# Mask products of an attention kernel moved from score tiles of their own into unused columns

## The chip, the cores and the metric

The kernel runs on one NeuronCore of a Trainium2 chip. The metric is the device time of one execution in microseconds (us), lower is better.

## What is computed

Three stages, one after the other, all in fp32:

```python
# attention: B, H, S, D = 2, 8, 768, 64, 16 centroids per head
q_assign = argmax(einsum('bhsd,hcd->bhsc', q_n, c_n))      # nearest centroid of each query
k_assign = argmax(einsum('bhsd,hcd->bhsc', k_n, c_n))      # and of each key
mask = q_assign[:, :, :, None] == k_assign[:, :, None, :]
scores = where(mask, q @ k.T / 8, -1e9)
attn = softmax(scores) @ v
# layer 1: 1536 tokens, 512 -> 2048 -> 512, a rational function between
# layer 2: 1536 tokens, 512 -> 1024 -> 512, softmax, normalisation between
```

Only the attention is touched by the change. A mask is made of the assignments: every query and every key gets a row of 16 zeros and ones (one-hot), and these rows are added to the operands of the score product, so that pairs of another cluster come out very low.

## The kernel before, in words

**Units.** The attention is a loop over 96 units (line 745): 16 heads n, 6 tiles of 128 queries t, idx = 6n + t. A unit makes its scores with four matmuls (L410 twice, L416 twice) in a PSUM tile `s` of two banks of 512 columns, of which it uses 384 each (`unit_scores`, L402). VectorE takes the minimum of each row (L421, called the max below, the sign being turned), ScalarE the exponential (L433, the exp below). At each odd unit VectorE transposes the exponentials of the two units before (L461, 1.77 us). TensorE multiplies them with v (L473); at t = 1 ScalarE copies the product of an earlier head out in two pieces (L491). The tiles `s` are a ring of two buffers: a unit's scores can be written when the tile two places earlier in the ring has been read out.

**Heads.** While head n runs, GpSimd prepares the operands of head n+1 (`prep_head`, L369 to L387): it needs the loads `dup` of that head (`load_head`, L213), issued on SP's queue at t = 3 of head n-1. At its fifth step SP copies the one-hot rows of the head into the operands (L386, L387).

**Masks.** They are made for sets of heads. Sets 0 and 1 are made at the start, sets 2, 3 and 4 (four heads each) inside the loop, by `assign` (L585), at the units listed in `SLOTS` (L105), after their queries and keys were loaded (`load_pairs`, L200, at the unit in `PAIRS`, L107: set 3 at unit 17, set 4 at 40). The steps of a set:

1. Three units hold the products with the centroids (L286) in columns 384 to 511 of their own score tiles, ahead of the scores; ScalarE copies them out after the exp of that unit (`keep`, L295).
2. `turn_in`: six transposes (L299) in a tile of their own; VectorE finds the maximum and compares (`is_max`, L305, L306).
3. `turn_back`: six bf16 transposes (L319) in a tile of their own; ScalarE copies 768 columns out (`back`, L323).
4. `first`: the product with a triangular matrix (L329) in a tile of its own; ScalarE copies 768 columns out (`to_rows`, L334), GpSimd turns half of the rows over (L336).

A tile of its own takes one place in the ring of two. Steps put in `pre` run on TensorE ahead of the unit's score matmuls, which are then ordered behind them (L407 to L414). `sums_out` (L511) also uses `pre`, at units 15, 27, 39, 51 and so on.

The instructions of an engine run in the order in which the program's scheduler has put them; `issue_after` and `behind` set parts of that order. Weights of the first layer are converted beside the attention (`to_f32`, L149 to L157): ScalarE's part for each piece comes every six units, at 29, 35, 41, 47, 53.

Of the kernel before, what the change touches and what calls it, by code (L numbers as in the profile page):

```python
# [7 lines left out]
F32 = mybir.dt.float32  # L8
F32R = mybir.dt.float32r
BF16 = mybir.dt.bfloat16  # L10
AF = mybir.ActivationFunctionType
ALU = mybir.AluOpType
# [3 lines left out]
B, H, S, D = 2, 8, 768, 64  # L16
C = 16
NT = S // 128
# [12 lines left out]
def fused_kernel(ctx: ExitStack, tc: tile.TileContext, qT, kT, v, cent, w1, w2i, w2o, gln, coef, centT, cst, tri, out):  # L31
    nc = tc.nc
# [14 lines left out]
    def psum2(tag, name):  # L47
        return ps[tag].tile([128, 2, 512], F32, name=name, tag=tag, bufs=2)
# [5 lines left out]
    def bank(tag, name):  # L54
        return stp.tile([128, 512], F32, name=name, tag=tag)
# [14 lines left out]
    trib = asp.tile([128, 128], BF16, name="trib")  # L70
    one = [asp.tile([128, 1], F32, name=f"one{i}") for i in range(2)]
# [30 lines left out]
    ACL = 67  # L102
    SET1 = (3, 5, 7)
    NBUSY = 15
    SLOTS = {2: (9, 10, 11, 12, 13, 15), 3: (24, 26, 28, 30, 31, 33), 4: (48, 50, 52, 54, 55, 57)}  # L105
    CONV, PARTS, SPLIT = 29, (69, 69, 81, 81, 87, 87, 89, 89, 93, 95), (39, 45, 63, 63)
    PAIRS = {17: 3, 40: 4}  # L107

    OLAG = 2

# [58 lines left out]
    def w1_f32(f):  # L169
        for a in range(2):  # L170
            o = slice(512 * a, 512 * a + 512)
            yield from to_f32(w1_f[f][:, o], w1[f, :, o], f"w1{f}{a}", True)

    def early_raws(f):
        for a in range(2):
            load_raw(w1[f, :, 512 * a:512 * a + 512], f"w1{f}{a}")
            yield
# [62 lines left out]
    t = bank("a0", "warm")  # L240
# [23 lines left out]
    MS, E, FV, FT, OH = {}, {}, {}, {}, {}  # L264

    def scales(k):
        es = sets[k]
        m = sm.tile([128, 3], F32, name=f"msc{k}", tag="msc", bufs=2)
        for j, (pp, i) in enumerate(es):
            if k < 1:  # L270
                nc.gpsimd.memset(m[32 * j:32 * j + 32, 0:1], 1.0 if i else -BIG)
                nc.gpsimd.memset(m[32 * j:32 * j + 32, 1:2], 0.0 if i else BIG)
            p = pp % 4
            (nc.vector if k < 1 else nc.gpsimd).tensor_copy(m[32 * j:32 * j + 32, 2:3], cnr[32 * p:32 * p + 32])
        OH[k] = qk.tile([128, S], F32R, name=f"oh{k}", tag="oh", bufs=2)
        for j, (pp, i) in enumerate(es):
            for h in range(2):
                mk[2 * pp + h, i] = OH[k][32 * j + 16 * h:32 * j + 16 * h + 16]
        MS[k] = m

    def sims(k, t0, nt, o):

        n = 128 * nt
        for j, (pp, i) in enumerate(sets[k]):
            p = pp % 4
            r = nc.tensor.matmul(o[32 * j:32 * j + 32], lhsT=cT[:, p * 32:(p + 1) * 32], rhs=raw["p", pp, i][:, t0 * 128:t0 * 128 + n])  # L286
        return r

    def keep(k, t0, nt, o):
        M = 32 * len(sets[k])  # L290
        if k not in E:
            E[k] = asp.tile([128, S], F32, name=f"sm{k}", tag="sm", bufs=2)
            FV[k] = asp.tile([128, NT, M], BF16, name=f"f{k}", tag=f"f{k > 1}", bufs=1 + (k < 2))
            FT[k] = E[k].bitcast(BF16)[:, 0:S]
        return nc.scalar.activation(out=E[k][0:M, t0 * 128:(t0 + nt) * 128].rearrange("p (a n) -> p a n", n=o.shape[2]), in_=o[0:M], func=AF.Copy, scale=MS[k][0:M, 2:3])  # L295

    def by_token(k, t, o):
        M = 32 * len(sets[k])
        return nc.tensor.transpose(o, E[k][0:M, t * 128:(t + 1) * 128], ident[0:M, 0:M])  # L299
# [18 lines left out]
    def mask_t(k, t, o):  # L318
        return nc.tensor.transpose(o, FV[k][:, t], identb)  # L319


    def back(k, o):
        nc.scalar.activation(out=FT[k][0:o.shape[0]], in_=o, func=AF.Copy)  # L323

    def first(k, o):

        M = 32 * len(sets[k])
        for a in range(2):
            nc.tensor.matmul(o[0:M, a, 0:384], lhsT=trib[0:M, 0:M], rhs=FT[k][0:M, 384 * a:384 * a + 384])  # L329

    def to_rows(k, o):

        M = 32 * len(sets[k])
        nc.scalar.activation(out=OH[k][0:M].rearrange("p (a n) -> p a n", a=2), in_=o[0:M], func=AF.Relu, scale=one[k > 1][0:M])  # L334
        q = OH[k][0:M // 2]
        nc.gpsimd.tensor_scalar(q, q.bitcast(F32), -1.0, 1.0, op0=ALU.mult, op1=ALU.add)  # L336
        masked[k] = S

    masked = dict.fromkeys(range(len(sets)), 0)
# [60 lines left out]
    pre, steps = {}, {}  # L400
# [39 lines left out]
    def step(u, e, f):  # L440
        steps.setdefault((u, e), []).append(f)
# [143 lines left out]
    def assign(k, us):  # L585

        w = {}

        def slot(i):
            w[i] = psum2("s", f"w{k}{i}")  # L590
            return w[i]

        def two_sims(c):
            def g(sp):
                w[c] = sp[:, :, 384:512]
                for t in range(2):
                    r = sims(k, 2 * c + t, 1, sp[:, t, 384:512])
                return r
            return g

        def turn_in():
            o = slot(3)
            for t in range(NT):
                by_token(k, t, o[:, t // 3, t % 3 * 128:t % 3 * 128 + 128])

        def turn_back():
            o = slot(4).bitcast(BF16)[:, 0]
            for t in range(NT):
                mask_t(k, t, o[:, t * 128:t * 128 + 128])

        step(us[0] - 1, "dve", lambda: scales(k))
        for c in range(3):
            pre[us[c]] = [two_sims(c)]
            step(us[c], "act", lambda c=c: keep(k, 2 * c, 2, w[c]))
        step(us[3], "pe", turn_in)
        step(us[3], "dve", lambda: is_max(w[3][:, :, 0:384], FV[k].rearrange("p (a t) m -> p a (t m)", a=2)))
        step(us[4], "pe", turn_back)
        step(us[4], "act", lambda: back(k, w[4].bitcast(BF16)[:, 0, 0:S]))
        step(us[5], "pe", lambda: first(k, slot(5)))
        step(us[5], "act", lambda: to_rows(k, w[5][:, :, 0:384]))  # L620

    scales(0)
    M = 32 * len(sets[0])
# [15 lines left out]
    for a in range(2):  # L639
        tps.append(bank(f"a{a}", f"set0{a}")[:, 0:3 * M].rearrange("p (t m) -> p t m", t=3))  # L640
        for t in range(3):
            r = by_token(0, 3 * a + t, tps[a][:, t])
        is_max(tps[a], EQ[:, 3 * a:3 * a + 3])
    t = bank("b1", "busy")
    for i in range(NBUSY):
        w = nc.tensor.matmul(t[:, 0:128], lhsT=z, rhs=z)
# [10 lines left out]
    for i in range(2):  # L657
        for a in (i, 1 - i):
            c = slice(384 * a, 384 * a + 384)
# [4 lines left out]
    for a in range(2):  # L664
        c = slice(384 * a, 384 * a + 384)
# [42 lines left out]
    for k in range(2, len(sets)):  # L708
        assign(k, SLOTS[k])
    for f in range(NPRE):  # L710
        w1_f[f] = wl0.tile([128, 1024], F32, name=f"w1f{f}", tag="l")
    for f in range(NPRE):
        g = w1_f32(f)
# [4 lines left out]
        g = early_raws(f)  # L718
        for a in range(2):
            planc[CONV - 6 + 12 * f + 6 * a].append(g)  # L720
        g = w1_parts(f)
# [23 lines left out]
    for idx, (n, t) in enumerate(units):  # L745
# [9 lines left out]
        with tc.issue_after(last["mk", n].ins) if n else ExitStack(), tc.issue_after(last["v"].ins) if n > 1 else ExitStack():  # L755
            if idx in PAIRS:
                load_pairs(sets[PAIRS[idx]])
            if t == 3 and 0 < n < B * H - 2:
                load_head(n + 2)
        sp = unit_scores(n, t)  # L760
# [313 lines left out]
    for f in (*range(NPRE, 16), *(16 + i for i in (0, 1, 2, 3, 6, 7, 4, 5))):  # L1074
        for a in range(2):
            if f < 16:
                to_load.append((w1[f, :, 512 * a:512 * a + 512], f"w1{f}{a}"))
            else:
                c = 2 * (f - 16) + a
# [93 lines left out]
```

## Time and profile before

| what | us |
|---|---|
| median of 3 runs | 635.71 (635.43 to 636.82) |
| the profiled execution, its own time | 632.73 |
| its span, first to last instruction | 630.9 |
| first exp of the 96 units starts | 17.09 |
| last exp of the 96 units starts | 211.13 |

Times in the rows are counted from the start of the span. A row of a timeline has start, duration, engine, line, operation, output and inputs, and in brackets how long the engine was idle before it and what ended that. Consecutive instructions of one group are one row with their count.

### The profile page before, as it was taken

The page shows a single profiled execution, that of the slowest core. Times are in us where ns is not written, and L with a number is a line of the kernel's source. Part 1 is how long each engine was busy: PE and PEld are TensorE (multiplying, and loading weights), DVE is VectorE, ACT ScalarE, POOL GpSimd, SP SyncE. Part 2 cuts the span into 40 slices and gives each one's busy share as a digit, 9 for nine tenths or more (in the row PEclk, how much of TensorE's full clock was granted, in tenths as well). Part 3 has the DMA queues.
Part 4 walks back from the last instruction along what each step waited for, and adds up shares of the span by engine and source line. Part 5 has one row for each costly group of instructions (what it writes and reads, how often), then busy time and mean ns, then how long its engine had stood idle before and what let it go on. Part 6 is the DMA issues. An engine that isn't in the chain of part 4 may idle for free.

```text
span 630.9 us, 13931 instructions
## 1 busy us (share of the span) xinstructions
PE 596.7 (95%) x5591; PEld 473.2 (75%) x5591; DVE 479.9 (76%) x633; ACT 444.2 (70%) x811; POOL 394.4 (63%) x338
## 2 busy tenths in 40 slices
PE   8789898989897999999999999999999999999997
PEld 5466666657675877888888888877888888888886
DVE  4888889989999798979889768689797554453450
ACT  4766678768787889899898787989794344443342
POOL 7845488788989679989989886888784000000000
PEclk9999999999999999999999999999999999999999
DMA  9948969977984523223313232221000000000001
GB/s 229 218 102 240 232 173 269 218 186 193 228 188 120 166 70 106 89 68 100 101 66 102 66 78 90 67 72 62 2 0 1 1 18 33 18 18 33 18 17 51
DMA packets 22585, 64.80 MB, mean 103 GB/s; under 512 B 4548, under 2 KB 5784, under 8 KB 22520
## 3 DMA queue, kind: packets, MB, share of 16 engines
q1 hardware_dynamic: 22088, 63.73, 37.3%
q8 instruction: 44, 0.72, 0.5%
q10 hardware_dynamic: 432, 0.17, 0.1%
q14 instruction: 21, 0.17, 0.1%
HBM read 59.23 MB, written 3.19 MB: 99 GB/s over the span
## 4 chain that ended last, share of the span: by engine, by line
PE 61%; POOL 11%; ACT 9%; DVE 8%; DMA 6%; issue 3%; SPq 2%; POOLq 0%; ACTq 0%; DVEq 0%
PE y L922 16%; PE h L815 15%; PE hh L1010 11%; PE o L1061 10%; DMA dup<-in_kT 4%; DVE m L421 2%; PE pv L473 2%; ACT p L433 2%; POOL k L377 2%; PE s L410 2%; POOL q L382 2%; PE lt L1043 2%; DMA raww<-in_w 1%; DVE pt L461 1%; PE s L416 1%
## 5 line engine op out<-in xcount | busy, mean ns | idle before, releaser
L433 ACT ACTIVATE p<-s,m 128x768 f32<-128x768 f32 x96 | 86.2, 900 | 49.4 <-DVE m L421 48.7
L815 PE MATMUL h<-xhl,w1h 128*128 128x512 f32 x336 | 106.5, 393 | 0.1
L421 DVE TENSOR_REDUCE m<-s 128x1 f32<-128x768 f32 x96 | 88.4, 941 | 17.1 <-PE s L416 17.1
L473 PE MATMUL pv<-pt,v 32*64 32x192 f32 x3072 | 81.0, 330 | 4.7 <-ACT w L491 4.7
L461 DVE STREAM_TRANSPOSE pt<-p 128x1536 f32<-128x1536 f32 (+1 forms) x49 | 84.9, 1732 | 0.2 <-ACT p L433 0.2
L905 POOL TENSOR_TENSOR gl<-y,gh 128x512 fp32r<-128x512 f32 x48 | 71.3, 1488 | 16.7 <-ACT gh L904 16.5
L473 PEld LDWEIGHTS pv<-pt,v 32*64 32x64 f32 x3072 | 57.9, 130 | 22.0 <-issue 13.5
L815 PEld LDWEIGHTS h<-xhl,w1h 128*128 128x128 f32 x336 | 62.8, 188 | 14.8 <-DVE y L899 0.5
L410 PE MATMUL s<-k,q 128*128 128x384 f32 x192 | 57.4, 381 | 12.7 <-ACT p L433 8.3
L922 PE MATMUL y<-gl,w1h 128*128 128x512 f32 x168 | 66.1, 393 | 1.3 <-POOL gl L905 1.3
L886 POOL TENSOR_TENSOR q<-q,t 128x512 f32<-128x512 f32 x48 | 64.4, 1343 | 2.9
L922 PE MATMUL y<-gh,w1l 128*128 128x512 f32 x168 | 65.8, 392 | 0.0
L815 PE MATMUL h<-xhl,w1l 128*128 128x512 f32 x168 | 65.6, 392 | 0.0
L922 PE MATMUL y<-gh,w1h 128*128 128x512 f32 x168 | 61.7, 392 | 0.0
L410 PEld LDWEIGHTS s<-k,q 128*128 128x128 f32 x192 | 29.3, 188 | 33.5 <-ACT p L433 16.2
L885 POOL TENSOR_SCALAR q<-t,ab 128x512 f32<-128x512 f32 x48 | 42.4, 884 | 17.9 <-ACT t L883 13.0
L1010 PE MATMUL hh<-vh,xhl 128*128 128x512 f32 x160 | 51.0, 395 | 0.0
L887 DVE TENSOR_TENSOR y<-y,h 128x512 f32<-128x512 f32 x48 | 32.8, 684 | 23.4 <-ACT y L884 23.1
L416 PE MATMUL s<-k,q 128*128 128x384 f32 x192 | 49.3, 338 | 0.3 <-DVE k L663 0.3
L897 DVE SCALAR_TENSOR_TENSOR q<-q,h 128x512 f32<-128x512 f32 x47 | 32.1, 682 | 11.7 <-ACT h L895 11.0
L922 PEld LDWEIGHTS y<-gl,w1h 128*128 128x128 f32 x168 | 31.5, 188 | 9.6 <-POOL gl L905 2.8
L904 ACT ACTIVATE gh<-y 128x512 fp32r<-128x512 f32 x48 | 30.0, 631 | 11.6 <-DVE y L899 11.5
(189 smaller groups left out, 1414.5 us busy)
## 6 DMA issues: line engine op xcount, KB each, us to landing
raww<-in_w SPq DMA_DIRECT2D x32, 512.0 KB, 3.6
v<-in_v SPq DMA_DIRECT2D x64, 192.0 KB, 4.1
dup<-in_qT SPq DMA_DIRECT2D x31, 192.0 KB, 5.9
dup<-in_kT SPq DMA_DIRECT2D x31, 192.0 KB, 5.9
rawv<-in_w2i SPq DMA_DIRECT2D x8, 512.0 KB, 3.5
rawv<-in_w2o SPq DMA_DIRECT2D x8, 512.0 KB, 3.7
out<-ob SPq DMA_DIRECT2D x11, 256.0 KB, 2.0
pr<-in_qT SPq DMA_DIRECT2D x7, 384.0 KB, 6.8
```

The lines of the kernel that those rows point to most:

```text
L410: r = nc.tensor.matmul(sp[:, a, 0:384], lhsT=q1[i][:, sl], rhs=k1[i][:, a * 384:(a + 1) * 384], start=True, stop=False)
L416: last["pe"] = nc.tensor.matmul(sp[:, a, 0:384], lhsT=q2[i][:, sl], rhs=k2[i][:, a * 384:(a + 1) * 384], start=False, stop=True)
L421: last["dve"] = nc.vector.tensor_reduce(m, sp[:, :, 0:384], axis=AX.XY, op=ALU.min)
L433: last["act"] = nc.scalar.activation(out=P[n, t // 2][:, t % 2], in_=sp[:, :, 0:384], func=AF.Exp, scale=-1.0, bias=m, accum_out=rs[key][: ...
L461: r = nc.vector.transpose(PT[n][:, 2 * i + m * a:2 * i + m * a + m].rearrange("p t k -> p (t k)"), p[:, m * a:m * a + m].rearrange("p t a ...
L473: last["pv"] = nc.tensor.matmul(pv[n][64 * c:64 * c + 64, r, 0:192].rearrange("p (t q) -> p t q", t=NT), lhsT=vv[n][sl, j], rhs=PT[n][sl, ...
L815: r = nc.tensor.matmul(hp, lhsT=w[:, kt * 128:(kt + 1) * 128], rhs=x[:, kt], start=(i == 0), stop=(i == 11))
L886: nc.gpsimd.tensor_tensor(q, q, t, op=ALU.mult)
L905: nc.gpsimd.tensor_tensor(gl, y, gh.bitcast(F32), op=ALU.subtract)
L922: nc.tensor.matmul(o, lhsT=w[:, c], rhs=g, start=(first and i == 0), stop=(last and i == 2))
L1010: last["th"] = nc.tensor.matmul(hp[:, a], lhsT=y[:, kt], rhs=w[:, 512 * a:512 * a + 512], start=(kt == 0 and e == 0), stop=(kt == 3 and e ...
L1061: r = nc.tensor.matmul(op[:, 0:m], lhsT=l[:, kt], rhs=w, start=(n == 0), stop=(n == 23))
```

## The change

`SLOTS` gets nine units for each set instead of six. The tile of its own stays for `turn_in` alone. The transposes back are made in the spare columns of two units (four and two transposes), the triangular products in those of three units (256 tokens each), all through `pre`, and each is copied out by ScalarE after the exp of its unit: two pieces instead of one, and three instead of one. Set 2 starts at the same unit as before, sets 3 and 4 two units earlier, and their pairs are loaded one unit earlier.

```diff
-    SLOTS = {2: (9, 10, 11, 12, 13, 15), 3: (24, 26, 28, 30, 31, 33), 4: (48, 50, 52, 54, 55, 57)}
+    SLOTS = {2: (9, 10, 11, 12, 13, 14, 16, 17, 18), 3: (22, 24, 26, 28, 29, 30, 31, 32, 33), 4: (46, 48, 50, 52, 53, 54, 55, 56, 57)}
...
-    PAIRS = {17: 3, 40: 4}
+    PAIRS = {16: 3, 39: 4}
...
-        def turn_back():
-            o = slot(4).bitcast(BF16)[:, 0]
-            for t in range(NT):
-                mask_t(k, t, o[:, t * 128:t * 128 + 128])
+        def turn_back(t0, n):
+            def g(sp):
+                w[t0, "b"] = sp.bitcast(BF16)[:, :, 768:1024]
+                for t in range(n):
+                    r = mask_t(k, t0 + t, w[t0, "b"][:, t // 2, t % 2 * 128:t % 2 * 128 + 128])
+                return r
+            return g
+
+        def first_of(c):
+            def g(sp):
+                w[c, "f"] = sp[:, :, 384:512]
+                for t in range(2):
+                    o = 256 * c + 128 * t
+                    r = nc.tensor.matmul(sp[:, t, 384:512], lhsT=trib, rhs=FT[k][:, o:o + 128])
+                return r
+            return g
+
+        def back_of(t0, n):
+            nc.scalar.activation(out=FT[k][:, 128 * t0:128 * (t0 + n)].rearrange("p (a n) -> p a n", n=256), in_=w[t0, "b"][:, 0:n // 2], func=AF.Copy)
+
+        def rows_of(c):
+            o = OH[k][:, 256 * c:256 * c + 256]
+            nc.scalar.activation(out=o.rearrange("p (a n) -> p a n", a=2), in_=w[c, "f"], func=AF.Relu, scale=one[1])
+            q = o[0:64]
+            nc.gpsimd.tensor_scalar(q, q.bitcast(F32), -1.0, 1.0, op0=ALU.mult, op1=ALU.add)
+            masked[k] += 256
...
-        step(us[4], "pe", turn_back)
-        step(us[4], "act", lambda: back(k, w[4].bitcast(BF16)[:, 0, 0:S]))
-        step(us[5], "pe", lambda: first(k, slot(5)))
-        step(us[5], "act", lambda: to_rows(k, w[5][:, :, 0:384]))
+        for i, (t0, n) in enumerate(((0, 4), (4, 2))):
+            pre[us[4 + i]] = [turn_back(t0, n)]
+            step(us[4 + i], "act", lambda t0=t0, n=n: back_of(t0, n))
+        for c in range(3):
+            pre[us[6 + c]] = [first_of(c)]
+            step(us[6 + c], "act", lambda c=c: rows_of(c))
```

## Rows read from the trace of the kernel before

**Rows 1.** The page: bytes moved in 40 slices of 15.8 us, the chain that ended last.

```profile
GB/s 229 218 102 240 232 173 269 218 186 193 228 188 120 166 70 106 89 68 100 101 66 102 66 78 90 67 72 62 2 0 1 1 18 33 18 18 33 18 17 51
...
PE 61%; POOL 11%; ACT 9%; DVE 8%; DMA 6%; issue 3%; SPq 2%; POOLq 0%; ACTq 0%; DVEq 0%
```

**Rows 2.** Timeline of ScalarE: the exps of units 31, 32, 33, 34, 35, 36, 37, 38.

```profile
81.39 0.90 ACT L433 ACTIVATE p<-s,m 128x768 f32<-128x768 f32 x1 [2.05 <-DVE m L421]
...
84.76 0.90 ACT L433 ACTIVATE p<-s,m 128x768 f32<-128x768 f32 x1
...
85.65 0.90 ACT L433 ACTIVATE p<-s,m 128x768 f32<-128x768 f32 x1
...
89.08 0.90 ACT L433 ACTIVATE p<-s,m 128x768 f32<-128x768 f32 x1 [1.65 <-DVE m L421]
...
90.42 0.90 ACT L433 ACTIVATE p<-s,m 128x768 f32<-128x768 f32 x1 [0.35 <-DVE m L421]
...
93.00 0.90 ACT L433 ACTIVATE p<-s,m 128x768 f32<-128x768 f32 x1 [0.37 <-DVE m L421]
...
94.09 0.90 ACT L433 ACTIVATE p<-s,m 128x768 f32<-128x768 f32 x1
...
96.75 0.90 ACT L433 ACTIVATE p<-s,m 128x768 f32<-128x768 f32 x1 [0.16 <-DVE m L421]
```

**Rows 3.** Timeline of VectorE at unit 30 and 31: the compare, the next max.

```profile
79.16 0.96 DVE L306 TENSOR_TENSOR f<-w,mx 128x768 bf16<-128x768 f32 x1
80.40 0.96 DVE L421 TENSOR_REDUCE m<-s 128x1 f32<-128x768 f32 x1 [0.28 <-PE s L416]
```

**Rows 4.** Timeline of TensorE: scores of units 30, 31, transposes back, scores of units 48, 54.

```profile
76.30 0.61 PE L410 MATMUL s<-k,q 128*128 128x384 f32 x2 [0.95 <-DMA dup<-in_kT]
...
79.40 0.62 PE L410 MATMUL s<-k,q 128*128 128x384 f32 x2 [1.48 <-ACT p L433]
...
81.09 0.51 PE L319 MATMUL w<-identb,f 128*128 128x128 bf16 x6
...
113.50 0.62 PE L410 MATMUL s<-k,q 128*128 128x384 f32 x2
...
127.19 0.61 PE L410 MATMUL s<-k,q 128*128 128x384 f32 x2 [1.24 <-POOL q L382]
```

**Rows 5.** Groups of instructions by form: count, busy us, mean ns, idle before.

```profile
L152 ACT ACTIVATE raww<-raww,less 128x512 uint32<-128x512 uint32 x32 | 24.6, 770 | 0.0
...
L491 ACT ACTIVATE w<-pv 64x768 f32<-64x768 f32 x16 | 12.9, 806 | 0.3
...
L149 ACT ACTIVATE w1f<-raww 128x512 f32<-128x512 f32 x10 | 6.6, 664 | 0.0
...
L1065 ACT ACTIVATE ob<-o 128x512 f32<-128x512 f32 x11 | 6.5, 593 | 14.2 <-PE o L1061 14.2
...
L295 ACT ACTIVATE sm<-s,msc 128x256 f32<-128x256 f32 x9 | 4.2, 466 | 0.0
...
L334 ACT ACTIVATE oh<-w,one 128x768 fp32r<-128x768 f32 x3 | 2.7, 893 | 0.0
...
L336 POOL TENSOR_SCALAR oh<-oh 64x768 fp32r<-64x768 f32 x3 | 2.5, 831 | 6.2 <-ACT oh L334 6.2
...
L323 ACT ACTIVATE sm<-w 128x768 bf16<-128x768 bf16 x3 | 2.4, 801 | 0.0
```

**Rows 6.** Tile pr, window 40 to 130: what TensorE waited for before L286 (us, times).

```profile
  ACT sm L295: 2.8, 6
```

**Rows 7.** The chain, window 14 to 150: load of head 8.

```profile
97.98 6.16 DMA dup<-in_kT
```

**Rows 8.** Timeline of SP's queue: first loads of pairs of set 4.

```profile
98.62 1.06 SPq L209 DMA_DIRECT2D pr<-in_qT  x2
```

**Rows 9.** Timeline of GpSimd: first and last instruction of the preparation of head 8.

```profile
104.28 0.91 POOL L363 TENSOR_SCALAR k<-dup,sgn 128x768 fp32r<-128x768 f32 x1 [2.37 <-DMA dup<-in_kT]
...
108.90 1.83 POOL L382 TENSOR_TENSOR q<-dup,q 64x768 fp32r<-64x768 f32 x1
```

## The prediction

> **What bounds the kernel now.** I read the page's chain first, to see which engines carry the end [rows 1]: TensorE has 61%, most of it in the two layers behind the attention, which the change doesn't touch and which start when the attention is done. The rest is the attention, where the chain changes hands between VectorE, ScalarE, GpSimd and loads. So the question is by how much the last unit ends earlier; the layers move with it.
>
> The second view is ScalarE's timeline, where the starts of the exps give the step from unit to unit [rows 2]. Without mask work a step from an odd to an even unit is 2.58 us (35 to 36) or 2.66 where an earlier product is copied out (37 to 38); the reader is to compare 3.37 (31 to 32) and 3.43 (33 to 34), the units behind which the transposes back and the triangular product take a tile of their own. The same steps stand at units 13 and 15, 55 and 57, so each of the three sets pays both. The third view is VectorE and TensorE around the compare [rows 3, 4], for what a matmul that needs the compare's result would wait for. The fourth is the start of heads 5 and 9 (units 30 and 54), where TensorE stands 0.95 and 1.24 us until the head's operands are there, which come late because their loads do [rows 4].
>
> **The sum, term by term.** All of it is against the profiled execution (632.73 us, span 630.9). The median shown is 3.0 us above that, so I work out a difference and take it from the median.
>
> A, the two tiles removed from the ring. Transposes back: 3.37 - 2.66 = 0.71 us. Triangular product: 3.43 - 2.58 = 0.85 [rows 2]. Three sets: **-4.7 us**. The third tile, for turn_in, stays, with VectorE's compare.
>
> B, a new wait. The transposes back now stand on TensorE ahead of the scores of the unit right behind the compare, and those scores are ordered behind them. Before, the next unit's scores needed only the exp: they began at 79.40 and the max at 80.40, while the compare ran until 79.16 + 0.96 = 80.12 [rows 3, 4]. Now TensorE waits for 80.12, makes four transposes (four sixths of 0.51 is 0.34) and then the scores, 1.0 us to the max as before: 81.5. VectorE's next max is 1.1 us later, and queued behind it are its transpose of the exponentials, and on TensorE the unit's products with v, so nothing slips into the gap. If something hid it, it would cost nothing; the bounds are 0 and 1.1 a set. I take the upper, as the rows show all three operations and no other work on VectorE: **+3.3 us**.
>
> C, ScalarE's smaller pieces. The triangular products come out as 3 x 0.466 for one of 0.893, +0.51; the transposes as about 0.59 (512 columns, by the nearest row) and 0.47 (256) for 0.80, +0.26 [rows 5]. That is 0.77 a set. Each piece also holds its unit's tile until it is done: TensorE (its weight loads counted apart) waited 6 times, 0.47 us each, for such copies of spare columns [rows 6]. Were each of the fifteen new copies paid like that, it would be 7.0 us, the upper bound; the lower is 0, where VectorE ends last. I take 0.5 a set, two thirds of ScalarE's growth: ScalarE ends last where the 0.81 us copies of the product with v fall (units 13, 31, 55), VectorE in the others. **+1.5 us**.
>
> D, the moved compare. In sets 3 and 4 turn_in goes from units 30 and 54 to 28 and 52, ahead of the two stalls. The extra time of the compare then passes while the loads are on their way, and up to 0.95 + 1.24 = 2.2 us of stall go [rows 4]. What is late next is ScalarE: between the exps of units 29 and 30 (53 and 54) lie its part of a weight conversion, 0.66 + 0.77 [rows 5], now a copy of 0.59, and the exp with its accumulator read, about 1.0: 3.0 us where 2.6 was the step, 0.4 each back. Net **-1.4 us**, between -2.2 and 0.
>
> E, the loads of pairs one unit earlier. At unit 39 this passes something: the pairs (4 x 393 kB = 1.57 MB) are now issued ahead of head 8's operands, not behind them as in [rows 7, 8]. At the 269 GB/s of that slice [rows 1] 1.57 MB are 5.8 us. Head 8's preparation began at 104.28, waiting for its load, and ended at 108.90 + 1.83 = 110.7 [rows 9]; unit 48's scores, which need it, began at 113.50 [rows 4], a slack of 2.8. So a load 5.8 us later costs 3.0 and one up to 2.8 later nothing. Before, the pairs were already on their way while head 8's load landed, 6.16 us after its last issue, so part of the 5.8 was paid then; I take a delay of 3.3, **+0.5 us**. At unit 16 the pairs pass no other load: nothing, covered by the six units until their first use; if they were late, unit 22's scores would stand behind them.
>
> F, at nothing: the centroid products of sets 3 and 4 move by two units, at the same price. GpSimd's turning over comes in three pieces for one of 0.83 us [rows 5]; it waited 6.2 us for ScalarE there, and the mask is ready by units 18, 33 and 57, three units or more before its rows are copied. If GpSimd were full there, a piece would cost some 0.3 us. VectorE's count of instructions stays.
>
> Sum: -4.7 + 3.3 + 1.5 - 1.4 + 0.5 = **-0.8 us**, 634.9 from the median. About 0.2% (1.3 us) is what a measurement of this kernel can tell from no change, so I forecast no difference that can be told.
>
> **A rule beside term C.** TensorE's waits for copies of spare columns show that a bank isn't written again before the copy has ended, though the columns differ [rows 6]. The Trainium skill, PSUM — Partial Sum Buffer, section "PSUM bank collisions raise a hardware error", says that two engines must be kept off one bank in the same partitions whatever the columns, so unused columns are no room beside the scores but a longer hold on the bank. The trace agrees that there is a wait. By the rule alone every copy is paid, C is 7.0 and the sum +4.7; by the rows' mix of waits and slack it is -0.8.
>
> **The rivals.** *The new wait is hidden (faster).* VectorE's max can slip behind the compare without loss if ScalarE, with its larger load in these units, ends last there anyway; then B is nearly nothing and A stands. For it: before the exps of units 32 and 33 ScalarE wasn't idle [rows 2]. Against: at unit 31 it stood 2.05 us for VectorE's max. With B at zero the sum is -4.1, 631.6; it decides from half of B on (-2.4, 633.3).
>
> *The load of head 8 is held up (slower).* If the transfers are taken strictly in their order, head 8's operands come the full 5.8 us later, its preparation ends at 116.5 and unit 48 waits 3.0 instead of 0.5: +2.5, so the sum is +1.7, 637.4. It decides from a delay of 5.4 us on, and from less where D gives little. For it: GpSimd already waited on that load, which took 6.16 us with only what was ahead of it [rows 7, 9]. Against: the pairs shared its time before, so not all of the 5.8 is new. The Trainium skill, DMA: Bandwidth & Descriptors, section "Queues, rings and completion order", says that each transfer engine consumes one queue's descriptors in ring order, which is this rival; the landing of one load in this trace can't tell it from sharing.
>
> *Every copy holds its bank on the path (slower).* C at its bound of 7.0 instead of 1.5: +5.5, sum +4.7, 640.4. Against: the steps 2.58 and 2.66 are VectorE's rate, and a buffer held 0.47 us longer is often free by then.
>
> **How the numbers follow.** The forecast, all terms near their values, within 0.2%: 0.39. Hidden wait: 0.38; A is the best measured term, and any half of B with it is enough. Head 8 held up: 0.18. Banks: 0.05. So faster 0.38, same 0.39, slower 0.23. Both signs hold most of the chance; the forecast's own range is 633.6 to 636.2. For 8 in 10 it reaches to most of the hidden wait, 632.0, and over the late load, 637.7.
>
> **What would show it.** Right: exp steps behind units 31 and 33 fall from 3.4 to 2.6 to 3.1; the step from 28 to 29 is about 4.2 (the 3.04 of 30 to 31 before, and 1.1), with VectorE idle some 1.4 us for scores; no TensorE stall at units 30 and 54. Wrong: the step 28 to 29 under 3.6 (B hidden), a TensorE wait of over 1 us for GpSimd at unit 48 (E), or ScalarE without a gap from unit 30 to 36 (C). If the last exp moves by more than 1.3 us from 211.13, or the layers behind don't move with it, the forecast is wrong.

## The result, and the profile after

The changed kernel takes 640.12 us (median of 7 runs, 638.46 to 642.71), the kernel before, on the same chip, 635.71 (632.85 to 638.87): a ratio of **1.0074, interval 1.0045 to 1.0103**, or about 4.7 us slower. No difference was forecast, and the point missed by 5.2 us. The profiled execution of after took 640.03 us (span 638.2), near its median; that of before was one of its quick ones, so the two traces differ by more (7.3 us) than the medians.

The page first: the line of the granted clock in 40 slices of the span (before, then after), and the chain of after.

```profile
PEclk9999999999999999999999999999999999999999
...
PEclk9989999889989999999999999999999999999999
PE 63%; DVE 14%; ACT 8%; POOL 5%; DMA 4%; issue 4%; SPq 1%; POOLq 0%; ACTq 0%; DVEq 0%
```

Against [rows 1], VectorE's share of the chain has grown from 8% to 14%. The compares of sets 2 and 4 stand in it now, but with some 3.7 us they are only 0.6% of the span; most of the rest is maxima and transposes. The clock shows 9 or more tenths in every slice of this execution of before, and falls in slices 3, 8, 9 and 12 of after; before_again, the same kernel as before, has one such slice, the second.

Next, ScalarE's timeline of after: the exps of units 28 to 35.

```profile
74.25 0.90 ACT L433 ACTIVATE p<-s,m 128x768 f32<-128x768 f32 x1 [1.09 <-DVE m L421]
78.31 0.90 ACT L433 ACTIVATE p<-s,m 128x768 f32<-128x768 f32 x1 [3.07 <-DVE m L421]
82.45 0.90 ACT L433 ACTIVATE p<-s,m 128x768 f32<-128x768 f32 x1 [1.47 <-DVE m L421]
83.61 0.90 ACT L433 ACTIVATE p<-s,m 128x768 f32<-128x768 f32 x1
86.63 0.90 ACT L433 ACTIVATE p<-s,m 128x768 f32<-128x768 f32 x1
87.88 0.90 ACT L433 ACTIVATE p<-s,m 128x768 f32<-128x768 f32 x1
90.10 0.90 ACT L433 ACTIVATE p<-s,m 128x768 f32<-128x768 f32 x1 [0.86 <-DVE m L421]
91.44 0.90 ACT L433 ACTIVATE p<-s,m 128x768 f32<-128x768 f32 x1 [0.35 <-DVE m L421]
```

The two steps that held the own tiles have shrunk as forecast: 31 to 32 takes 3.02 us (3.37 in [rows 2]) and 33 to 34 2.22 (3.43). The step from 28 to 29 is 4.06 (4.2 was forecast). But 29 to 30 takes 4.14, where the forecast had the stall for the head's load gone. TensorE's timeline of after shows what ended five of its longest waits, at units 13, 29, 30, 48 and 53:

```profile
41.24 0.61 PE L319 MATMUL s<-identb,f 128*128 128x128 bf16 x4 [2.12 <-DVE f L306]
...
76.14 0.40 PE L319 MATMUL s<-identb,f 128*128 128x128 bf16 x4 [1.53 <-DVE f L306]
...
80.39 0.62 PE L410 MATMUL s<-k,q 128*128 128x384 f32 x2 [1.41 <-POOL q L382]
...
118.83 0.62 PE L410 MATMUL s<-k,q 128*128 128x384 f32 x2 [2.50 <-POOL q L382]
...
131.91 0.40 PE L319 MATMUL s<-identb,f 128*128 128x128 bf16 x4 [1.83 <-DVE f L306]
```

Three waits for the compare were expected. Units 30 and 48, 1.41 and 2.50 us, wait for a head's preparation on GpSimd, and that in turn for loads. For unit 30, follow SP's queue and GpSimd some 20 us upstream. The kernel before, rows not shown so far (SP's queue, then GpSimd):

```profile
57.95 0.54 SPq L386 DMA_DIRECT2D k<-oh  x1
58.61 0.53 SPq L387 DMA_DIRECT2D q<-oh  x1
59.25 2.22 SPq L227 DMA_DIRECT2D v<-in_v  x4
...
49.43 0.83 POOL L336 TENSOR_SCALAR oh<-oh 64x768 fp32r<-64x768 f32 x1 [6.24 <-ACT oh L334]
54.43 0.91 POOL L363 TENSOR_SCALAR k<-dup,sgn 128x768 fp32r<-128x768 f32 x1 [4.17 <-DMA dup<-in_kT]
...
69.97 0.91 POOL L363 TENSOR_SCALAR k<-dup,sgn 128x768 fp32r<-128x768 f32 x1 [5.28 <-DMA dup<-in_kT]
```

And after: the queue's wait (us in total, times, longest), the queue, GpSimd.

```profile
SPq L387 <- POOL oh L630: 2.6, 1, 2.6
...
59.09 0.54 SPq L386 DMA_DIRECT2D k<-oh  x1
62.34 0.53 SPq L387 DMA_DIRECT2D q<-oh  x1
62.98 2.96 SPq L227 DMA_DIRECT2D v<-in_v  x4
...
52.57 0.40 POOL L630 TENSOR_SCALAR oh<-oh 64x256 fp32r<-64x256 f32 x1 [9.77 <-ACT oh L628]
55.17 0.91 POOL L363 TENSOR_SCALAR k<-dup,sgn 128x768 fp32r<-128x768 f32 x1 [2.21 <-DMA dup<-in_kT]
...
59.62 1.84 POOL L382 TENSOR_TENSOR q<-dup,q 64x768 fp32r<-64x768 f32 x1
61.55 0.77 POOL L630 TENSOR_SCALAR oh<-oh 64x256 fp32r<-64x256 f32 x2
...
74.07 0.91 POOL L363 TENSOR_SCALAR k<-dup,sgn 128x768 fp32r<-128x768 f32 x1 [7.91 <-DMA dup<-in_kT]
```

Before, set 2's rows were turned over at 49.43, ahead of head 4's preparation. After, they are whole two to three units later, and the last two of GpSimd's three pieces stand behind that preparation, at 61.55. The copy q<-oh needs them and is in SP's queue; the loads of v and of head 5's operands are queued behind it. They go out 3.7 us later (62.98 for 59.25; 1.1 of it is there already at the copy k<-oh ahead of them), and head 5's preparation begins at 74.07 for 69.97. This was in no term of the sum. The runs had to say what it is worth.

### The profile page after: what moved, and what is told of

Its sections match the earlier page's. It is cut to its first block, busy times and chain, and to the rows that moved or that the text cites. A ratio compares the mean times of both kernels' runs of the same rounds, so it can differ in the third digit from the quotient of the medians.

```text
span 638.2 us, 13973 instructions
## 1 busy us (share of the span) xinstructions
PE 601.3 (94%) x5603; PEld 477.4 (75%) x5603; DVE 481.5 (75%) x633; ACT 445.1 (70%) x820; POOL 394.8 (62%) x344
## 4 chain that ended last, share of the span: by engine, by line
PE 63%; DVE 14%; ACT 8%; POOL 5%; DMA 4%; issue 4%; SPq 1%; POOLq 0%; ACTq 0%; DVEq 0%
PE y L946 16%; PE h L839 15%; PE hh L1034 10%; PE o L1085 10%; DVE m L421 4%; DVE pt L461 3%; DMA dup<-in_kT 3%; PE pv L473 3%; PE s L410 3%; ACT p L433 2%; PE s L416 2%; PE lt L1067 2%; DMA v<-in_v 1%; POOL gl L929 1%; POOL q L910 1%
## 5 line engine op out<-in xcount | busy, mean ns | idle before, releaser
L473 PE MATMUL pv<-pt,v 32*64 32x192 f32 x3072 | 82.7, 340 | 6.4 <-ACT w L491 5.2
L473 PEld LDWEIGHTS pv<-pt,v 32*64 32x64 f32 x3072 | 59.9, 136 | 24.1 <-issue 14.7
L410 PE MATMUL s<-k,q 128*128 128x384 f32 x192 | 58.8, 389 | 9.5 <-POOL q L382 4.3
L416 PE MATMUL s<-k,q 128*128 128x384 f32 x192 | 50.4, 345 | 0.3 <-DVE k L687 0.3
```

The lines of the kernel that those rows point to most:

```text
L410: r = nc.tensor.matmul(sp[:, a, 0:384], lhsT=q1[i][:, sl], rhs=k1[i][:, a * 384:(a + 1) * 384], start=True, stop=False)
L416: last["pe"] = nc.tensor.matmul(sp[:, a, 0:384], lhsT=q2[i][:, sl], rhs=k2[i][:, a * 384:(a + 1) * 384], start=False, stop=True)
L473: last["pv"] = nc.tensor.matmul(pv[n][64 * c:64 * c + 64, r, 0:192].rearrange("p (t q) -> p t q", t=NT), lhsT=vv[n][sl, j], rhs=PT[n][sl, ...
```

## The experiments

All ratios are to the kernel before run beside them on one chip; 0.001 is 0.63 us. Executions differ by 2 to 3 us in how loads fall, so single traces say where, ratios how much.

**Wait and load order (first runs).** e1_pairs40 loads set 4's pairs at unit 40, as before; e2_only_pairs is the kernel before with the pairs of both sets one unit earlier, set 3's at 16 and set 4's at 39. The edit of e1_pairs40:

```diff
-    PAIRS = {16: 3, 39: 4}
+    PAIRS = {16: 3, 40: 4}
```

> The changed kernel with the pairs of set 4 loaded at unit 40 again, behind head 8's operands; nothing else is undone. Load order theory (the loss is the 1.57 MB put ahead of head 8's load): the step from unit 47 to 48 falls from 5.82 us to about 3.0, GpSimd's wait before head 8's preparation from 6.1 to under 3 us, and the time by 3 to 4.5 us, to 635.6 to 637. New wait theory (the loss is TensorE's wait for the compare and the lower granted clock behind it): unit 48 costs at most 1 us of it, time 639 or more.

> The kernel before with only the loads of pairs moved one unit earlier (units 16 and 39). Load order theory: 3 to 4.5 us slower than before, with a stall of TensorE at unit 48 of 2 us or more. New wait theory: within 1 us of before.

Measured: 1.0054 (1.0025 to 1.0083) and 1.0027 (0.9998 to 1.0056). The earlier load costs 1.3 us in the one (less than the load order theory had, more than the other) and 1.7 in the other, not settled by either interval alone. In after the chain shows head 8's load, its last issue landing 8.85 us later, and GpSimd its preparation:

```profile
103.50 8.85 DMA dup<-in_kT
```
```profile
112.53 0.91 POOL L363 TENSOR_SCALAR k<-dup,sgn 128x768 fp32r<-128x768 f32 x1 [6.12 <-DMA dup<-in_kT]
```

That is 8.2 us after 104.28 [rows 9] (the loads of v ahead of it, at 95.11 for 94.08, were 1.0 us late already), and unit 48 stood 2.50 us for it. With the pairs back at 40 GpSimd begins that preparation without a wait, and the step from 47 to 48 is 3.01 (after 5.82, before 3.01).

e3_gap leaves one unit between the compare and the transposes back; e4_gap_pairs40 has both edits.

```diff
-    SLOTS = {2: (9, 10, 11, 12, 13, 14, 16, 17, 18), 3: (22, 24, 26, 28, 29, 30, 31, 32, 33), 4: (46, 48, 50, 52, 53, 54, 55, 56, 57)}
+    SLOTS = {2: (9, 10, 11, 12, 14, 16, 17, 18, 19), 3: (22, 24, 26, 28, 30, 31, 32, 33, 34), 4: (46, 48, 50, 52, 54, 55, 56, 57, 58)}
```

> The changed kernel with one unit left free between the compare and the first transposes back (units 14, 16; 30, 31; 54, 55; the triangular products three units further on as before), so that no unit's scores stand behind the compare; loads as in the changed kernel. New wait theory: the step behind the compare falls from 4.0 to 4.85 us to about 3.05, granted clock 1.0 there, and the time falls by 3 to 4 us, to 636 to 637. Load order theory: the wait was mostly slack ahead of late loads; time within 1.5 us of the changed kernel, the stall at unit 48 stays.

> Both edits together. If the two causes add up, 6 to 8 us below the changed kernel, 632.5 to 634, faster than before by 0.3 to 0.5%. If each only uncovers the other, no more than the better one of the two alone, 635.6 to 637.

Measured: 1.0023 (1.0000 to 1.0047) and 1.0005 (0.9977 to 1.0034). The gap gives back 3.2 us against after and 3.1 against e1_pairs40; the steps 12 to 13 and 28 to 29 fall from 4.85 and 4.06 to 3.05 and 3.04. The wait is real, at the size of term B. From e3_gap to e4_gap_pairs40 the pairs are worth 1.1 us. But with both costs gone the kernel only equals before, where the sum without B and E has -4.6 us.

The kernel before, run again unchanged, shows what such a comparison resolves: 0.9997 (0.9973 to 1.0021).

> The kernel before once more, against itself, for the spread of its runs and a second profile. Every theory: a ratio of 1.000 within 0.003; the steps at the masks as in the first profile; where two executions of the same kernel differ, the difference is in waits for loads, not in the steps at the masks.

e5_busy adds four matmuls of zeros into unused columns ahead of the four transposes back, to keep TensorE at work in its wait.

```diff
+                if t0 == 0:
+                    for _ in range(4):
+                        nc.tensor.matmul(sp[:, 1, 384:512], lhsT=z, rhs=z)
```

> The changed kernel with four matmuls of zeros written into the spare columns ahead of the four transposes back, so that TensorE stands still for about 1 us less behind the compare (the zeros are overwritten; the mask is unchanged). Clock theory (the wait costs twice, as the granted clock falls to half behind it): granted clock 1.0 behind the compares of sets 2 and 4, steps there back to about 4.05 us from 4.85 at set 2, time 1.5 to 3 us below the changed kernel. Wait theory alone: no change within 1 us, as the wait itself stays.

Measured: 1.0062 (1.0031 to 1.0093), 0.8 us under after, less than the intervals tell apart. The clock stayed at 1.00 from 40 to 50 us (0.83 in after) and the step from 12 to 13 fell from 4.85 to 4.21: a local gain, no verdict on the whole.

e6_gap_late (with the gap) and e7_late (without) are the changed kernel with sets 3 and 4 begun at 24 and 48, as before; the diff is e7_late's, against the changed kernel. In e6_gap_late set 2 is as in e3_gap, and in sets 3 and 4 all that follows the compare is a unit later than in e7_late.

```diff
-    SLOTS = {2: (9, 10, 11, 12, 13, 14, 16, 17, 18), 3: (22, 24, 26, 28, 29, 30, 31, 32, 33), 4: (46, 48, 50, 52, 53, 54, 55, 56, 57)}
+    SLOTS = {2: (9, 10, 11, 12, 13, 14, 16, 17, 18), 3: (24, 26, 28, 30, 31, 32, 33, 34, 35), 4: (48, 50, 52, 54, 55, 56, 57, 58, 59)}
...
-    PAIRS = {16: 3, 39: 4}
+    PAIRS = {17: 3, 40: 4}
```

> One unit free behind the compare, as in the run with the gap, and all else of sets 3 and 4 at the old times: their compares at units 30 and 54, pairs loaded at 17 and 40. If moving the compare ahead of the stalls was worth the 1.4 us of the prediction, this is 1 to 2 us slower than the run with gap and pairs at 40, 635 to 636; if it was worth nothing, the same, 633.5 to 634.5.

> The changed kernel with sets 3 and 4 at the old times (compares at units 30 and 54, transposes back right behind, at 31 and 55, pairs loaded at 17 and 40): the new wait without the new order of loads and without the moved compare. Wait theory: 2 to 4 us slower than the run with the gap at the old times, since only the unit behind the compare differs. If the wait only showed because it stood ahead of head 9's late load, the two are the same.

Measured: 1.0062 (1.0035 to 1.0089) and 1.0100 (1.0061 to 1.0138). The early dates are worth 3.6 and 2.9 us (against e4_gap_pairs40 and e1_pairs40), twice what term D took. Between these two the gap gives 2.4 us, a third value for the wait. And at the old dates, without wait or load order, the change is still 3.9 us slower than before.

**Which part eats the gain.** move_only takes the early dates alone, first_only the products alone, back_only the transposes back alone (with a gap). The last two load their pairs as before, at 17 and 40. move_only's edit is against the kernel before; of the other two, the lines that they put into the changed kernel are shown, without those that they replace.

```diff
-    SLOTS = {2: (9, 10, 11, 12, 13, 15), 3: (24, 26, 28, 30, 31, 33), 4: (48, 50, 52, 54, 55, 57)}
-    PAIRS = {17: 3, 40: 4}
+    SLOTS = {2: (9, 10, 11, 12, 13, 15), 3: (22, 24, 26, 28, 29, 31), 4: (46, 48, 50, 52, 53, 55)}
+    PAIRS = {16: 3, 40: 4}
```
```diff
+    SLOTS = {2: (9, 10, 11, 12, 13, 15, 16, 17), 3: (24, 26, 28, 30, 31, 33, 34, 35), 4: (48, 50, 52, 54, 55, 57, 58, 59)}
...
+        step(us[4], "pe", turn_back)
...
+            pre[us[5 + c]] = [first_of(c)]
```
```diff
+    SLOTS = {2: (9, 10, 11, 12, 14, 16, 17), 3: (24, 26, 28, 30, 32, 33, 34), 4: (48, 50, 52, 54, 56, 57, 58)}
...
+            pre[us[4 + i]] = [turn_back(t0, n)]
...
+        step(us[6], "pe", lambda: first(k, slot(6)))
```

> The kernel before with only the two dates moved: sets 3 and 4 begin two units earlier (22 and 46 instead of 24 and 48), pairs of set 3 at 16, of set 4 still at 40, own tiles kept, both queues of loads as before. Theory (term D, the moved compare is a real gain: the pairs of runs with and without it differ by 2.9 and 3.6 us): faster by 1.4 to 3.6 us, ratio 0.994 to 0.998, and no TensorE stall on the load at units 30 and 54 that stands behind the compare. Rival (the difference came from other stalls of those runs, since later heads' loads set the pace either way): within 1 us, ratio 0.9985 to 1.0015.

> The kernel before with only the triangular products moved into spare columns of three units (15 to 17, 33 to 35, 57 to 59), in three ScalarE pieces and three GpSimd pieces; the transposes back keep a tile of their own and all dates are those of before. Theory (term A holds for this half, 0.85 us a set, less half of term C): faster by 1.5 to 2.5 us, ratio 0.996 to 0.998. Rival (what ate the gain of the whole is the product's half: the smaller ScalarE pieces, and rows that are whole only two units later than before, so that head 8's and head 10's operands and GpSimd's last piece come late): slower by 1 to 4 us, ratio 1.002 to 1.006, with new stalls of TensorE in the units after 36 and 60.

> The kernel before with only the transposes back moved into spare columns of two units, with one unit between the transposes in and the first of them (14 and 16, 32 and 33, 56 and 57); the triangular product keeps a tile of its own in the next unit; sets begin at the dates of before. Theory (term A holds for this half, 0.71 us a set): faster by 1 to 2 us, ratio 0.997 to 0.9985. Rival (what ate the gain of the whole is this half: the scores' tile is held by the copy back): slower by 1 to 3 us, ratio 1.0015 to 1.005, with longer steps behind units 14, 16, 32, 33, 56 and 57.

> The kernel after with a unit of gap behind the transposes in and the pairs of set 4 loaded at unit 40, the same kernel that measured 1.0005 [0.9977, 1.0034]. Theory (wait and load order are the whole excess of the change): 0.998 to 1.002 again. Rival (the spare columns cost something by themselves that a favourable batch hid): 1.003 to 1.006.

Measured: move_only **0.9964** (0.9933 to 0.9994), 2.3 us faster; first_only **1.0079** (1.0057 to 1.0101), 5.0 slower; back_only 1.0017 (0.9991 to 1.0043), where the rival begins and outside what the theory had, but not told apart from no change; e4_again 1.0004 (0.9978 to 1.0031), as the first time. In first_only the steps behind 15 and 33 did fall, from 3.43 to 2.59 and 2.50, so the gain was there; the loss came later, and SP's waits and TensorE's timeline name it:

```profile
SPq L387 <- POOL oh L627: 8.6, 1, 8.6
```
```profile
72.50 0.53 PE L473 MATMUL pv<-pt,v 32*64 32x192 f32 x2 [0.97 <-DMA v<-in_v]
```

Here only set 2's last piece fell behind head 4's preparation. The queue had come to that copy early and stood 8.6 us there; the copy went out at 62.61, 4.0 us later than before, and the loads of v at 66.62, 7.4 later. The step from 27 to 28 took 7.89 us (2.79 before): TensorE waited for v, and from 76 to 80 us its granted clock was 0.50.

**Is it the late rows, or the spare columns?** vec2_after and vec2_e4 are after and e4_gap_pairs40 with set 2's pieces turned over on VectorE; old_set2 is e4_gap_pairs40 with set 2 alone back in its own tiles, at 13 and 15.

```diff
-            nc.gpsimd.tensor_scalar(q, q.bitcast(F32), -1.0, 1.0, op0=ALU.mult, op1=ALU.add)
+            (nc.vector if k == 2 else nc.gpsimd).tensor_scalar(q, q.bitcast(F32), -1.0, 1.0, op0=ALU.mult, op1=ALU.add)
```
```diff
+        if k == 2:
+            step(us[4], "pe", turn_back_own)
+            step(us[4], "act", lambda: back(k, w[4].bitcast(BF16)[:, 0, 0:S]))
+            step(us[5], "pe", lambda: first(k, slot(5)))
+            step(us[5], "act", lambda: to_rows(k, w[5][:, :, 0:384]))
+            return
```

> The kernel after, but the three pieces of set 2 are turned over on VectorE and not on GpSimd, so that the first copy of mask rows no longer waits behind a head's preparation. Theory (the loading queue standing 2.6 us at that copy delays the head's loads behind it and so the later units): the queue's wait for the turned rows is gone, unit 30 has no TensorE stall on its head, and the time falls by 1.5 to 3.5 us against the kernel after, less about 0.9 us of VectorE: ratio to before 1.003 to 1.006 (after: 1.0074). Rival (the spare columns cost by themselves, the queue's wait is covered): 1.007 to 1.010, the VectorE work on top.

> The kernel with the gap behind the compare and the pairs of set 4 at unit 40 (twice 1.0005), its set 2 turned over on VectorE. Theory (the queue's wait at the copy of mask rows eats the gain): ratio 0.995 to 0.998, no wait of the loading queue for turned rows, the step from unit 29 to 30 back from 5.2 to 5.9 us to under 4. Rival (the spare columns cost by themselves): 1.000 to 1.003.

> The same kernel with the gap and the pairs of set 4 at unit 40, but set 2 alone in its old form: transposes back and triangular product in tiles of their own at units 13 and 15, rows whole at unit 15; sets 3 and 4 keep the spare columns. Theory (late rows of set 2 are what eats the gain): the removed tiles of sets 3 and 4 and the moved dates stay, ratio 0.993 to 0.997, as the moved dates alone (0.9964) or better. Rival (spare columns cost in every set): 0.998 to 1.002, no better than with set 2 in spare columns.

Measured: 1.0072 (1.0045 to 1.0099), 0.9972 (0.9944 to 0.9999), and **0.9938** (0.9915 to 0.9961). vec2_e4 is 2.1 us under its own GpSimd version. vec2_after's ratio fell into the rival's range; yet both lost the queue's wait (0.4 us and none) and the stall at unit 30: the step from 29 to 30 is 2.59 and 2.63, for 4.14 in after and 5.90 in e4_again. What vec2_after gained there it paid on VectorE, in units 12 to 20 (21.85 us for 19.21). Its three pieces:

```profile
53.18 0.29 DVE L630 TENSOR_SCALAR oh<-oh 64x256 fp32r<-64x256 f32 x1 [1.48 <-ACT oh L628]
...
55.95 0.24 DVE L630 TENSOR_SCALAR oh<-oh 64x256 fp32r<-64x256 f32 x1
...
59.54 1.66 DVE L630 TENSOR_SCALAR oh<-oh 64x256 fp32r<-64x256 f32 x1
```

The third took seven times the second; the last section comes back to it.

Step by step, set 2 answers the question. e4_again and old_set2 differ in set 2 alone. Its spare columns stand in units 14 to 19, and the exps of units 12 and 20 enclose them. Before, then e4_again:

```profile
39.78 0.90 ACT L433 ACTIVATE p<-s,m 128x768 f32<-128x768 f32 x1 [1.23 <-DVE m L421]
...
57.91 0.90 ACT L433 ACTIVATE p<-s,m 128x768 f32<-128x768 f32 x1
```
```profile
41.25 0.90 ACT L433 ACTIVATE p<-s,m 128x768 f32<-128x768 f32 x1 [1.23 <-DVE m L421]
...
58.84 0.90 ACT L433 ACTIVATE p<-s,m 128x768 f32<-128x768 f32 x1
...
80.68 1.01 PE L410 MATMUL s<-k,q 128*128 128x384 f32 x2 [2.38 <-POOL q L382]
```

That is 18.13 us before (18.11 and 18.12 in before_again and old_set2) and 17.59 in e4_again (17.59 to 17.61 in the other three runs with the gap and GpSimd's pieces). In their own units set 2's spare columns gain 0.5 us, and up to unit 29 nothing of it is lost. The loss stands at one place, the step from 29 to 30: 5.90 us in e4_again and 5.23 in e4_gap_pairs40, 2.63 in old_set2, where TensorE has no wait for head 5's preparation. In e4_again all three pieces stand behind head 4's preparation, SP's queue waits 3.0 us for them, and TensorE 2.38 us at unit 30.

The last three runs: late_rows is the kernel before with set 2's last two tiles at units 16 and 18; late_turn is the kernel before with one GpSimd instruction, set 2's turning over, moved behind head 4's preparation; old_set2_again repeats old_set2.

```diff
-    SLOTS = {2: (9, 10, 11, 12, 13, 15), 3: (24, 26, 28, 30, 31, 33), 4: (48, 50, 52, 54, 55, 57)}
+    SLOTS = {2: (9, 10, 11, 12, 16, 18), 3: (24, 26, 28, 30, 31, 33), 4: (48, 50, 52, 54, 55, 57)}
```
```diff
+        if k != 2:
+            turn_over(k, M)
...
+        if n == 4:
+            with tc.issue_after(lastq.ins):
+                turn_over(2, 32 * len(sets[2]))
```

> The kernel before, all tiles its own, no spare columns for transposes back or products; only set 2's transposes back move from unit 13 to 16 and its triangular product from 15 to 18, so that its rows are whole at unit 18 and GpSimd turns them behind a head's preparation. No other date and no order of loads changes. Theory (late rows hold the loading queue and with it the later heads' loads): the queue waits 2 to 4 us for the turned rows, the step from unit 29 to 30 grows, slower by 2 to 4.5 us, ratio 1.003 to 1.007. Rival (it was the spare columns of set 2 themselves): within 1 us, 0.9985 to 1.0015.

> The kernel before with one instruction moved: GpSimd turns set 2's rows over behind the five instructions of the preparation of the fifth head (as in the kernel after), not ahead of them. Everything else, each engine's order and the loading queue's, is as before. In late_rows the two tiles at units 16 and 18 cost 2.3 us in their own steps, so that run couldn't tell; this one can. Theory (the loading queue's wait for the turned rows delays the head's loads behind it): the queue waits 1.5 to 3 us at the first copy of mask rows, the loads behind it begin as much later, the step from unit 29 to 30 grows by 0.5 to 2.5 us; ratio 1.001 to 1.004. Rival (the wait is covered and only the placement of the work counts): no difference, 0.9985 to 1.001, the step from 29 to 30 unchanged.

> The same kernel as old_set2 (0.9938 [0.9915, 0.9961]): sets 3 and 4 in spare columns with a gap and early dates, set 2 in its own tiles. If that was its level: 0.992 to 0.9965 again; if a favourable batch: 0.997 to 1.000.

Measured: late_rows 1.0070 (1.0043 to 1.0097), late_turn **1.0081** (1.0051 to 1.0110), old_set2_again 0.9954 (0.9930 to 0.9978). late_rows has the ratio that the theory expected, and its queue waits 2.1 us, but its profile puts 2.3 us of the loss into units 12 to 20 themselves, and its step from 29 to 30 is 2.65: it can't carry the point. late_turn can. The same instructions stand in the same order on every engine and in the loading queue, but for that one; its units up to 23 keep their steps. SP's wait, then GpSimd's piece, then TensorE's timeline:

```profile
SPq L394 <- POOL oh L340: 3.0, 1, 3.0
```
```profile
60.86 0.83 POOL L340 TENSOR_SCALAR oh<-oh 64x768 fp32r<-64x768 f32 x1
```
```profile
65.38 0.59 PE L423 MATMUL s<-k,q 128*128 128x384 f32 x2 [1.12 <-DMA q<-oh]
...
80.11 0.62 PE L417 MATMUL s<-k,q 128*128 128x384 f32 x2 [3.21 <-DMA dup<-in_kT]
```

TensorE now waits 1.12 us at unit 24 for the rows, and 3.21 at unit 30 for head 5's operands where it was 0.95 [rows 4]: the step from 29 to 30 is 5.74 us (3.46 before). Of 4.5 us that this execution has lost by unit 32, 1.4 stand at the step from 23 to 24, which is the rows' own reader, 2.3 at 29 to 30 and 0.85 at 31 to 32. The whole is 5.1 us slower, more than the 0.4% at most that the theory expected, for one piece of 0.83 us that stands in another place.

## Why the prediction was wrong

**The step that failed is F.** It put GpSimd's turning over at nothing, because GpSimd had waited 6.2 us for ScalarE there [rows 5] and the mask would be ready by unit 18, "three units or more before its rows are copied". The idle time was real, all of it ahead of set 2's piece (6.24 us, above), but it lay ahead of head 4's preparation, and what comes later stands behind that: GpSimd is taken by 6.3 us of preparation (55.17 to 61.46). More idle time alone would not have helped: in after ScalarE has copied the second piece out at 53.49, and GpSimd does nothing until 55.17, waiting for the preparation's load, because in its order the piece comes behind:

```profile
53.02 0.47 ACT L628 ACTIVATE oh<-s,one 128x256 fp32r<-128x256 f32 x1
```

And the first reader of the rows isn't the matmul some units on but a copy in the loading queue, whose place there is fixed, with the next head's loads behind it. I asked what hides the piece, and not what is queued behind whoever waits for it. Two of the prediction's own signs of a wrong forecast came: the last exp of after starts at 218.96 for 211.13, and unit 48 waits 2.50 us for GpSimd.

The sum as the runs give it is a ladder whose rungs differ in one thing each: early dates alone -2.3 us (move_only, with set 3's pairs a unit earlier); sets 3 and 4 into spare columns with a gap -1.1 (to old_set2's mean of two, 0.9946); set 2 into spare columns with its rows late +3.7 (to e4_gap_pairs40); no gap +3.1 (to e1_pairs40); pairs ahead of head 8's loads +1.3 (to after). Together +4.7, which is no check, as each rung begins where the last one ends. Each rung is uncertain by about 2 us, so -1.1 and +1.3 alone could be nothing. The sum had -1.1 for set 2 (its share of A and C) where the ladder has +3.7: of the 5.5 us between -0.8 and +4.7, 4.8 stand there, and late_turn alone, without any spare column, loses 5.1.

- **A and C, the tiles and the smaller pieces: right in sign, C too small.** At set 2, with the gap, the steps behind units 13 and 15 fall by 0.67 and 1.15 us, 1.8 where A had 1.6. Those behind 14, 16, 18 and 19 grow by 0.48, 0.09, 0.36 and 0.37, 1.3 where C had 0.5. That leaves -0.5 for a set, half of the sum's -1.1. By halves, units 12 to 20 take 17.30 us in first_only and 18.09 in back_only (18.13 before): the gain is the triangular product's, the transposes back give none (the two don't add up exactly to the whole). For sets 3 and 4 together the sum had -2.1 and the ladder has -1.1.
- **The rival of every copy on the path** forecast 640.4, and 640.12 was measured, as the rule beside term C has +4.7 and the ladder ends at +4.7. That is luck. With every copy paid, C is 2.3 a set, and set 2 would have lost by its spare columns; it gained 0.5, and the loss came at other places.
- **B, the wait behind the compare: right**, 3.3 forecast, 3.1, 3.2 and 2.4 measured. In place it is 1.0 us each at sets 3 and 4, and 1.6 at set 2, where the clock fell too (units 12 to 20 take 19.21 us in after, 17.59 with the gap). The rival that it is hidden, which had nearly the same chance, falls.
- **D, the early dates: right in sign**, 1.4 forecast, 2.3 measured alone. In after its best place, unit 30, was lost to F.
- **E, the pairs: under-sized**, 0.5 forecast, 1.3, 1.7 and 1.1 measured. The rival with 2.5 had the mechanism: unit 48 stood 2.50 us for GpSimd, the sign of a wrong E that the prediction named. The Trainium skill, DMA: Bandwidth & Descriptors, section "Queues, rings and completion order", has each transfer engine take one queue's descriptors in ring order; the trace agrees in that with 1.57 MB ahead of it head 8's last load landed 8.85 us after its issue, 6.16 before [rows 7]. It was a second failure, not the one that turned the result: with E at 1.7 the sum would have been +0.4.

What stays open: how much of set 2's loss each delayed reader makes. late_turn loses 1.4 us at the rows' own reader and 3.1 at head 5's start and behind it; in e4_again nearly all stands at head 5's start. vec2_e4 gets 2.1 us back, and pays VectorE 1.6 in units 12 to 20 (19.17 for 17.59). Single executions differ too much to divide it further.

The version that beats both kernels is old_set2: spare columns for sets 3 and 4, a unit of gap behind the compare, set 2 as before. It measured 0.9938 and 0.9954, 3 to 4 us faster than the kernel before.

## What to carry to other kernels

When work is spread over more units, its result is whole later: look for its first reader, and if that is a queue that also carries loads, price the wait at all that is queued behind it, and not at the reader's own need alone. Idle time of an engine counts only where the moved instruction will stand in its order, and that order was read too late here. To size such an edit, move one instruction alone: late_turn said more than the versions that moved several things.

## What the runs showed of the hardware that was not expected

**The granted clock fell behind some of TensorE's waits and not behind others, and the length of the wait didn't tell which.** Windows of after (start and end, length, busy time of PE, PEld, DVE, ACT and POOL, clock, DMA share, GB/s):

```profile
38.00:41.00 3.00, 1.07 (x8) 0.64 (x6) 2.97 (x4) 1.37 (x4) 2.92 (x3) 0.98 0.02 6
41.00:44.00 3.00, 2.76 (x32) 2.23 (x40) 0.91 (x2) 0.00 (x0) 1.59 (x5) 0.50 0.02 5
...
74.00:78.00 4.00, 2.47 (x65) 1.85 (x72) 2.73 (x4) 0.99 (x2) 3.93 (x4) 1.00 0.97 202
```

Behind the wait of 2.12 us at unit 13 the clock was 0.50, the lower of the two levels, for some 3 us; behind that of 1.53 at unit 29 it stayed full. At unit 30 it fell in e4_again, behind 2.38 us, and stayed full in late_turn, behind 3.21:

```profile
80.00:84.00 4.00, 3.32 (x18) 2.58 (x26) 0.97 (x2) 0.58 (x1) 1.89 (x3) 0.57 0.59 190
```
```profile
80.00:84.00 4.00, 2.41 (x14) 2.00 (x14) 2.78 (x3) 0.99 (x2) 1.91 (x4) 1.00 0.41 130
```

Behind the same wait of 1.83 us at unit 53 it fell in after and not in e1_pairs40, and TensorE's 64 products with v next to it took 2.86 and 1.56 us. After, then e1_pairs40, each with its window's row:

```profile
131.00:137.00 6.00, 5.09 (x79) 4.09 (x80) 3.49 (x3) 2.77 (x6) 3.91 (x4) 0.72 0.61 151
...
132.99 2.86 PE L473 MATMUL pv<-pt,v 32*64 32x192 f32 x64
```
```profile
128.00:134.00 6.00, 4.17 (x96) 3.06 (x95) 4.72 (x5) 2.32 (x5) 4.07 (x3) 1.00 0.88 214
...
130.49 0.40 PE L319 MATMUL s<-identb,f 128*128 128x128 bf16 x4 [1.83 <-DVE f L306]
...
131.57 1.56 PE L473 MATMUL pv<-pt,v 32*64 32x192 f32 x64
```

So a wait can cost a further 1.3 us behind it, which term B had not priced; what decides whether it does, these runs don't show.

**VectorE's small elementwise piece took 1.66 us beside GpSimd, and 0.24 to 0.29 alone** (vec2_after, above). GpSimd had nothing to do until 56.69; at 59.54 it was in the tensor products of the preparation (L377, 59.24 to 61.05), and VectorE's piece ended 0.15 us after the first of them. vec2_e4 repeats this: two pieces took 2.31 us from 56.29 on, beside the same product (56.61 to 58.45), and ended 0.15 us after it. In vec2_after VectorE's max over 768 columns beside the next tensor product kept its 0.9 us. The Trainium skill, SBUF — State Buffer, section "Who interferes with whom", says that VectorE and GpSimd share a pair of ports which one instruction holds whole, that a tensor_scalar can need it and that a reduce doesn't. The trace agrees, with these numbers.
